# Row statistics on ScalarE, twelve more units turned by VectorE, and weight pieces placed later, in a fused top-k attention and MLP kernel

## The chip, the cores and the metric

The kernel runs on one core of one Trainium2 chip. The metric is the device time of one execution in microseconds (us); the time of a kernel is the median of several runs. A core has TensorE (PE, matmuls into the PSUM banks), VectorE (DVE), ScalarE (ACT), GpSimd (POOL) and SyncE (SP, which here issues nearly all DMAs). Each engine works through its own instructions in the order in which the program issues them, and waits on semaphores for the others.

## What is computed

The inputs are q, k and v of shape (8, 8, 576, 64), a gain g_ln of 512, and two weight matrices, 512 x 2048 and 2048 x 512, which arrive as 64-bit floats. Cut to what matters, the reference is:

```python
scores = q @ k.T / sqrt(64)
kth = np.partition(scores, -32, axis=-1)[..., -32:-31]
scores = np.where(scores >= kth, scores, -1e9)
attn = softmax(scores)
x = heads_side_by_side(attn @ v)              # (8, 576, 512)
mu = np.mean(x, axis=-1, keepdims=True)
var = np.mean((x - mu) ** 2, axis=-1, keepdims=True)
xn = (x - mu) / np.sqrt(var + 1e-06) * g_ln
out = x + np.maximum(xn @ w_ch1, 0.0) @ w_ch2
```

So each query keeps its 32 best keys. Everything is done in 32-bit floats.

## The kernel before

**Units and steps.** A job is one pair of heads of one batch with some of its query tiles; four query tiles have 128 rows and the rest tile has 64. A unit is one query tile of one job: a whole unit holds both heads' scores, 128 x 576 each, and a rest unit puts both heads' 64 rows on one 128 x 576 tile. There are 128 whole and 32 rest units. The main loop (L1201) makes one step per unit, and a few more at the end. In step n the program issues, in this order and to the queues of all engines: scores of unit n + 2 (`scores`, L373: PE matmuls L398, ScalarE copies L379), the selection of unit n on VectorE in four rounds of maxima and replacements (`select`, L422, with L441, L427, L433), the mask of unit n - 1 (`mask`, L487: ScalarE L490, then GpSimd's subtraction L493), its exponentials with their sums (`weigh`, L495: ScalarE L501), the turning of an older unit's weights, and values, projections and weights as they come due. At the end of a step `halve` (L407) makes the larger and the smaller half of the next unit's scores on VectorE (L419, L420), which the selection works on, and `watch` (L456) has GpSimd note a doubt in the selection (L460).

**The early steps.** In the steps up to 8 the mask and the exponentials of unit n - 1 are both in step n, and its transposes right behind them. `values` (L620: PE, L625 and L632) stands before the scores while n is at most `gives_first`, which is 9, and after them later (L1222, L1228).

**Turning.** The weights of a unit have to stand with keys on the partitions before they meet v. Either PE transposes them (L559, eight 128 x 128 transposes for a whole unit, with ScalarE's copies L571 out of PSUM), or the unit is "moved" (`move`, L527): VectorE transposes 32 x 32 blocks (L532, two instructions), one DMA writes the result to HBM and, in the step after, four DMAs bring it back into `pt` in the right places (`bring`, L538). 88 units are moved: from the fifth job on, all whole units but the last of their group. The last 64 keys of each unit, the "end keys", are always turned by PE (`turn_ends`, L582 to L592, and a ScalarE copy L602); for a moved unit this happens in step i + 3, right behind the scores and values of that step (L1232). The tiles e that hold the weights have two buffers, so the mask of a later unit waits for these transposes.

**The MLP.** A pair of 128-row tiles of x is a block; there are 18, two of them of rest rows. When a block's attention is complete, `give` (L1149) puts its work into the list `todo`: `rows` (transposes of x, L729), `hidden` (L770) and `project` (L809 in the first block, L927 in the others). `fill` (L269), called eight times a step, pops items from the list as a planned share per call allows; an item at the front that may not run yet holds up all behind it. The planner (`slot`, L1159) spreads what is left evenly over the steps up to coming blocks and keeps a reserve of 4 us for the moment at which a block is given. The last six items left at that moment are put behind the new rows (`at_end`, L1154).

**Statistics.** `Block.stats` (L689) makes each tile's mean and variance on VectorE (L695, L696). In the first block VectorE also subtracts the mean (L698); in the others GpSimd negates it (L701) and adds it (L704). The row may be transposed from the next step on (`centred`, L707). Tiles are done in the step after their last values, behind round 2 of the selection.

**Weights.** The 64-bit weights come in 32 pieces of 128 x 512 (16 for each matrix; `Piece`, L122). A piece is fetched (`fetch`), split (`split`: ScalarE L163, L165, L168, GpSimd's clamp L164 and, for the first matrix, the gain L170), shifted (`shift`: VectorE L176) and joined (`join`: GpSimd L182, L184). `batches` (L200) says which pieces belong to which step: four before the loop, then two and one in turn in steps 0 to 7, none in 8 and 9, two in each of 10 to 17. `weights(n, phase)` (L209) fetches the next step's pieces and splits the first of this step's early in the step; it joins the last step's and splits the second at the end of the step, or, from step 7 on (`LAZY`), in the middle, where the shift stands ahead of it. The first block may use a piece from the step after its join.

Of the kernel before, what the change touches and what calls it, by code (L numbers as in the profile page):

```python
# [29 lines left out]
def compute(  # L30
# [91 lines left out]
    class Piece:  # L122
# [26 lines left out]
        def split(self):  # L149
            i = self.i  # L150
            high = self.raw[:, :, 1].bitcast(FP32)
            if i < NF:
                self.size = hpool.tile([P, DM], U32, tag="h", name="size")[:]
                self.low = wt_rows[:, i % 8]
                homes = ((opool, "o"), (opool, "o"), (rpool, "r"), (rpool, "r"), (xtpool, "xT"))
            else:
                self.size = wt_rows[:, 2 * i % 8].bitcast(U32)
                self.low = wt_rows[:, (2 * i + 1) % 8]
                homes = ((opool, "o"), (opool, "o"), (rpool, "r"))
# [41 lines left out]
    queue = list(pieces)  # L201
    for n in range(-1, NF + 2):
        count = 4 if n < 0 else 1 + (n + 1) % 2 if n < NF // 2 else 0 if n < NF // 2 + 2 else 2
        batches[n], queue = queue[:count], queue[count:]
    assert not queue

    LAZY = 7

    def weights(n, phase):  # L209

        now, before = batches.get(n, []), batches.get(n - 1, [])
        if phase == 0:
            for x in batches.get(n + 1, []):
                x.fetch()
            for x in now[0::2]:
                x.split()
        elif phase == 1:
            for x in before:  # L220
                x.join()
            for x in now[1::2]:
                x.split()

# [38 lines left out]

    loads, sends = Later(), Later()
    brings = {}

    def fill(least=0):  # L269
        tick[0] += 1  # L270
        loads.settle(LOAD_AGE)
        sends.settle(SEND_AGE)
        ends_later.settle(END_AGE)
        fetch_forms(FETCH_AGE)
        owed[0] = min(owed[0] + share[0], 6.0)
        while todo and (not todo[0][3] or todo[0][3]()):
            if owed[0] < todo[0][1] / 2 and least <= 0:
                break
            least -= 1
            pop()  # L280
# [398 lines left out]
    class Block:  # L679
# [9 lines left out]
        def stats(self, i):  # L689
            x = self.x[i]  # L690
            if self.mv is None:
                self.mv = small.tile([P, J, 2], FP32, tag="mv", name="mv")
                self.rstd = small.tile([P, J], FP32, tag="rstd", name="rstd")
            st = brief_small.tile([P, 6], FP32, tag="st", name="st")
            nc.vector.bn_stats(out=st[:], in_=x)  # L695
            nc.vector.bn_aggr(out=self.mv[:, i, :], in_=st[:])  # L696
            if now[0] <= gives_first:
                nc.vector.tensor_scalar_sub(x, x, self.mv[:, i, 0:1])  # L698
            else:
                less = brief_small.tile([P, 1], FP32, tag="less", name="less")  # L700
                nc.gpsimd.tensor_scalar(  # L701
                    less[:], self.mv[:, i, 0:1], -1.0, 0.0, ALU.mult, ALU.add
                )
                nc.gpsimd.tensor_scalar(x, x, 1.0, less[:], ALU.mult, ALU.add)  # L704
            self.step[i] = now[0]

        def centred(self, i):  # L707
            return i in self.step and (now[0] <= gives_first or done(self.step[i]))

# [246 lines left out]
    SUM_AGE, END_AGE, FETCH_AGE, STORE_AGE, LOAD_AGE = 7, 6, 10, 8, 3  # L956
    SEND_AGE = 2
    blocks = []
# [89 lines left out]

    for u in units[EARLY:]:
        u.moved = not u.rest and u is not u.group.units[-1]  # L1050

# [97 lines left out]
    def give(n):  # L1149
        early = not all(map(done, ready))  # L1150
        for blk in gives[n]:
            rows, hidden, project = blk.items()

            at_end = 0 if early else 6  # L1154
            kept, last = todo[: len(todo) - at_end], todo[len(todo) - at_end :]
            assert all(t[0] == "project" for t in last)
            todo[:] = kept + rows + last + hidden + project
# [43 lines left out]
    for n in range(END):  # L1201
# [19 lines left out]
        ahead = due(n) if n else []  # L1221
        if g and n <= gives_first:  # L1222
            values(g)
        if quick:
            take_values(g)
        for x in ahead:
            scores(x)
        if g and n > gives_first:  # L1228
            values(g)
        if n in brings:  # L1230
            brings.pop(n)()
            late_ends = turn_ends(at(n - 3))  # L1232
        if u:
# [23 lines left out]
        if not early:  # L1257
            weights(n, 0)
        fill()
        if mk and not early:  # L1260
            prepare(mk)
# [153 lines left out]
```

## Time and profile before

| | us |
|---|---|
| median of 3 runs | 1619.47 (1617.36 to 1622.83) |
| the profiled execution | 1617.56 |
| its span | 1615.8 |
| PE busy | 1486.2 (92%) |
| VectorE busy | 1397.4 (86%) |
| GpSimd busy | 1084.7 (67%) |
| ScalarE busy | 1076.2 (67%) |

The profile is of one execution. The span runs from the first instruction to the last, and the execution's own time stands 1.8 us above it. Busy times are sums over the span; an engine's idle time costs something only where that engine sets the pace. Matmuls are pipelined and their ends are modelled, so PE's pace is better read from the times at which matmuls start than from their durations. A 32-bit matmul appears as two instructions, a transpose as one. Lines such as L770 are lines of the kernel before.

### The profile page before, as it was taken

The page shows a single profiled execution, that of the slowest core. Times are in us where ns is not written, and L with a number is a line of the kernel's source. Part 1 is how long each engine was busy: PE and PEld are TensorE (multiplying, and loading weights), DVE is VectorE, ACT ScalarE, POOL GpSimd, SP SyncE. Part 2 cuts the span into 40 slices and gives each one's busy share as a digit, 9 for nine tenths or more (in the row PEclk, how much of TensorE's full clock was granted, in tenths as well). Part 3 has the DMA queues.
Part 4 walks back from the last instruction along what each step waited for, and adds up shares of the span by engine and source line. Part 5 has one row for each costly group of instructions (what it writes and reads, how often), then busy time and mean ns, then how long its engine had stood idle before and what let it go on. Part 6 is the DMA issues. An engine that isn't in the chain of part 4 may idle for free.

```text
span 1615.8 us, 27078 instructions
## 1 busy us (share of the span) xinstructions
PE 1486.2 (92%) x7770; PEld 1124.1 (70%) x7770; DVE 1397.4 (86%) x3971; ACT 1076.2 (67%) x2984; POOL 1084.7 (67%) x1489
## 2 busy tenths in 40 slices
PE   3548978899989899999999999999999999999997
PEld 1335536567757677777777777777777777778886
DVE  7877879999999999999999999999999999982000
ACT  5776776676767686777776767677677776763311
POOL 6984887866647576777766768586767675756334
PEclk9768989899989999999999999999999999999999
DMA  8423455553656455545564556446564455522211
GB/s 214 128 75 115 146 154 124 173 159 115 189 140 189 127 159 155 172 146 145 163 189 135 142 137 189 153 131 169 136 189 150 130 163 160 167 81 86 70 36 54
DMA packets 367205, 228.27 MB, mean 141 GB/s; under 512 B 248772, under 2 KB 337352, under 8 KB 367048
## 3 DMA queue, kind: packets, MB, share of 16 engines
q1 hardware_dynamic: 362312, 225.86, 48.5%
q8 instruction: 64, 1.05, 0.3%
q10 hardware_dynamic: 4736, 0.59, 0.2%
q14 instruction: 93, 0.76, 0.2%
HBM read 154.01 MB, written 72.35 MB: 140 GB/s over the span
## 4 chain that ended last, share of the span: by engine, by line
PE 73%; POOL 10%; DVE 7%; ACT 6%; DMA 2%; issue 1%; SPq 0%; POOLq 0%; ACTq 0%; DVEq 0%
PE hps L770 27%; PE ops L927 22%; PE scps L398 9%; PE av L625 7%; POOL e L493 3%; PE tp L559 3%; PE av L632 2%; DVE m L441 2%; DVE hi L427 2%; POOL w L184 2%; ACT sc L379 1%; ACT e L490 1%; PE tp L729 1%; ACT e L501 1%; POOL wt L182 1%
## 5 line engine op out<-in xcount | busy, mean ns | idle before, releaser
L493 POOL TENSOR_TENSOR e<-e,sc 128x576 f32<-128x576 f32 x288 | 419.7, 1475 | 352.9 <-ACT e L490 352.5
L770 PE MATMUL hps<-xT,w 128*128 128x256 f32 x2304 | 544.0, 386 | 0.7 <-ACT xT L732 0.7
L770 PEld LDWEIGHTS hps<-xT,w 128*128 128x128 f32 x2304 | 429.7, 193 | 69.5 <-issue 11.8
L441 DVE MAX8 m<-hi 128x8 f32<-128x296 f32 (+1 forms) x1152 | 470.9, 444 | 0.1
L427 DVE MATCH_REPLACE8 hi<-m,hi 128x288 f32<-128x288 f32 (+1 forms) x864 | 378.0, 443 | 0.0
L927 PE MATMUL ops<-w,h 128*128 128x256 f32 x1360 | 323.1, 384 | 0.0
L501 ACT ACTIVATE e<-e,m 128x576 f32<-128x576 f32 x288 | 224.3, 779 | 119.0 <-POOL e L493 117.5
L927 PEld LDWEIGHTS ops<-w,h 128*128 128x128 f32 x1360 | 253.0, 193 | 37.9 <-issue 4.2
L379 ACT COPY sc<-scps 128x288 f32<-128x288 f32 x576 | 199.4, 407 | 101.4 <-PE scps L398 68.5
L490 ACT ACTIVATE e<-sc,m 128x576 f32<-128x576 f32 x288 | 212.3, 770 | 47.8 <-PE tp L592 47.8
L420 DVE TENSOR_TENSOR lo<-sc 128x576 f32<-128x576 f32 (+1 forms) x160 | 167.6, 1048 | 0.0
L419 DVE TENSOR_TENSOR hi<-sc 128x576 f32<-128x576 f32 (+1 forms) x160 | 142.9, 893 | 12.2 <-POOL watched L460 8.3
L625 PE MATMUL av<-pt,vb 128*64 128x256 f32 (+2 forms) x1088 | 147.0, 411 | 4.9 <-ACT r L644 4.3
L793 ACT ACTIVATE h<-hps 128x512 f32<-128x512 f32 x144 | 85.6, 595 | 80.4 <-PE hps L770 80.1
L532 DVE STREAM_TRANSPOSE sc<-e 128x512 f32<-128x512 f32 x176 | 114.3, 686 | 25.6 <-ACT e L501 25.6
L398 PE MATMUL scps<-kT,late_qT 64*128 64x288 f32 (+3 forms) x832 | 124.8, 413 | 7.5 <-ACT x L644 4.2
L927 PE MATMUL ops<-wt,s 128*128 128x256 f32 x544 | 128.6, 381 | 0.0
L559 PE MATMUL tp<-ident,e 128*128 128x128 f32 x448 | 75.7, 297 | 53.3 <-ACT e L501 53.3
L625 PEld LDWEIGHTS av<-pt,vb 128*64 128x64 f32 x1088 | 75.3, 141 | 62.2 <-issue 11.5
L433 DVE MAX8 hi<-lo 128x8 f32<-128x288 f32 x288 | 117.8, 445 | 0.0
L398 PEld LDWEIGHTS scps<-kT,late_qT 64*128 64x128 f32 (+1 forms) x832 | 70.4, 169 | 61.5 <-issue 23.8
L398 PE MATMUL scps<-kT,qT 64*128 64x288 f32 x512 | 92.8, 460 | 21.0 <-DVE qT L328 11.6
(104 smaller groups left out, 1893.4 us busy)
## 6 DMA issues: line engine op xcount, KB each, us to landing
turned<-sc SPq DMA_DIRECT2D x88, 512.0 KB, 2.8
pt<-turned SPq DMA_DIRECT2D x352, 128.0 KB, 2.8
w<-forms SPq DMA_DIRECT2D x136, 256.0 KB, 4.2
vb<-in_v_dram SPq DMA_DIRECT2D x68, 288.0 KB, 3.8
raw<-in_moe_w_ch_dram SPq DMA_DIRECT2D x32, 512.0 KB, 4.7
kT<-kept SPq DMA_DIRECT2D x36, 288.0 KB, 3.4
kin<-in_k_dram SPq DMA_DIRECT2D x128, 72.0 KB, 2.5
kept<-kT SPq DMA_DIRECT2D x32, 288.0 KB, 3.0
```

The source lines that it names most:

```text
L379: nc.scalar.copy(u.sc[:, t, s * HALF : (s + 1) * HALF], made[s][t][:, 0:HALF])
L398: nc.tensor.matmul(ps[i * R : i * R + ql, o : o + width], qT[r, q0 : q0 + ql], kT[r, k0 : k0 + width], start=True, stop=True,)
L419: nc.vector.tensor_tensor(hi, a, b, ALU.max)
L420: nc.vector.tensor_tensor(lo, a, b, ALU.min)
L427: nc.vector.match_replace(x, m[:, t, :], x, LOWEST)
L441: nc.vector.max(m[:, t, :], u.hi[:, t, 0:width])
L490: nc.scalar.activation(u.e[:, t], u.sc[:, t], AF.Relu, bias=u.edge[:, t : t + 1], scale=-STEEP)
L493: nc.gpsimd.tensor_tensor(u.e[:, t], u.e[:, t], u.sc[:, t], ALU.subtract)
L501: nc.scalar.activation(u.e[:, t], u.e[:, t], AF.Exp, bias=u.bias[:, t : t + 1], scale=-scale, accum_out=g.den[:, col : col + 1],)
L625: nc.tensor.matmul(av[h * D : (h + 1) * D, 0 : g.nq], vb[:, h * (J + 1) + c, :], g.blocks[:, h, 0 : g.nq // 32, c, :], start=(c == 0), sto ...
L770: nc.tensor.matmul(ps[0][:, side * N : (side + 1) * N], w1[:, c, f * P : (f + 1) * P], self.xT[:, c, 0:N], start=(c == 0), stop=(c == NC - 1),
L927: nc.tensor.matmul(bank[name][:, 0:Q], a(j), rhs, start=first and j == 0, stop=(j == G - 1), skip_group_check=not first,)
```

## The change

It has five parts.

1. **Statistics.** From the second block on, ScalarE copies the tile onto itself while it sums it (into the place of the variance), multiplies the sum by 1/512 to the mean, and, five fills later, squares the centred tile into a PSUM bank while it sums the squares, and multiplies that sum by 1/512. GpSimd subtracts the mean in one instruction. A row may be transposed six fills after its statistics were issued, in place of the next step.
2. **Turning.** The last whole unit of a group without a rest unit is moved too, from the third batch on, for every other pair of heads, if the next job does not begin with a rest unit: 12 units more, 100 in all.
3. **Weight pieces.** One piece a step in steps 0 to 7, none in 8, one in 9, then two a step in 10 to 18, and the last in 19. From step 9 on (`LATE`) a step's pieces are all split at the end of the step, behind shift and join of the last step's, and the next step's are fetched behind that. The shift stands right before the join in all steps, at the end. The last four pieces of the first matrix use the same homes for their parts as those of the second.
4. **Order on PE.** Values stand behind the scores in all steps but that of the first block's last group. The end keys of a moved unit are turned behind the first fill of the step.
5. **Rows.** Ten remaining items instead of six are put behind a new block's rows.

```diff
@@ split
-            if i < NF:
+            if i < 3 * NC:
@@ batches
-    for n in range(-1, NF + 2):
-        count = 4 if n < 0 else 1 + (n + 1) % 2 if n < NF // 2 else 0 if n < NF // 2 + 2 else 2
+    for n in range(-1, NF + 4):
+        count = 4 if n < 0 else 1 if n < NF // 2 else 0 if n == NF // 2 else 1 + (n > 9)
         batches[n], queue = queue[:count], queue[count:]
-    LAZY = 7
+    LATE = NF // 2 + 1
     def weights(n, phase):
         now, before = batches.get(n, []), batches.get(n - 1, [])
+        coming = batches.get(n + 1, [])
         if phase == 0:
-            for x in batches.get(n + 1, []):
+            for x in coming if n < LATE else []:
                 x.fetch()
-            for x in now[0::2]:
+            for x in now[0::2] if n < LATE else []:
                 x.split()
         elif phase == 1:
             for x in before:
+                x.shift()
+            for x in before:
                 x.join()
-            for x in now[1::2]:
+            for x in now if n >= LATE else now[1::2]:
                 x.split()
+            for x in coming if n >= LATE else []:
+                x.fetch()
@@ fill
         sends.settle(SEND_AGE)
+        squares.settle(SQUARE_AGE)
@@ Block.stats
+            mean, var = self.mv[:, i, 0:1], self.mv[:, i, 1:2]
             if now[0] <= gives_first:
                 st = brief_small.tile([P, 6], FP32, tag="st", name="st")
                 nc.vector.bn_stats(out=st[:], in_=x)
                 nc.vector.bn_aggr(out=self.mv[:, i, :], in_=st[:])
                 nc.vector.tensor_scalar_sub(x, x, mean)
             else:
-                nc.gpsimd.tensor_scalar(
-                    less[:], self.mv[:, i, 0:1], -1.0, 0.0, ALU.mult, ALU.add
-                )
-                nc.gpsimd.tensor_scalar(x, x, 1.0, less[:], ALU.mult, ALU.add)
-            self.step[i] = now[0]
+                nc.scalar.activation(x, x, AF.Copy, accum_out=var)
+                nc.scalar.mul(mean, var, 1.0 / DM)
+                nc.gpsimd.tensor_scalar(x, x, 1.0, mean, ALU.mult, ALU.subtract)
+                def square():
+                    ps = brief("squares")
+                    nc.scalar.activation(ps[:], x, AF.Square, accum_out=var)
+                    nc.scalar.mul(var, var, 1.0 / DM)
+                squares.add(square)
+            self.step[i] = tick[0]
@@ centred
-            return i in self.step and (now[0] <= gives_first or done(self.step[i]))
+            return i in self.step and (
+                now[0] <= gives_first or tick[0] - self.step[i] >= CENTRE_AGE
+            )
-    SEND_AGE = 2
+    SEND_AGE, CENTRE_AGE, SQUARE_AGE = 2, 6, 5
@@ which units are moved
-    for u in units[EARLY:]:
-        u.moved = not u.rest and u is not u.group.units[-1]
+    for j, nj in zip(jobs, jobs[1:] + [None]):
+        for u in units[max(j.first, EARLY) : j.last + 1]:
+            u.moved = not u.rest and (
+                u.i < j.last or (j.b > 1 and j.hp % 2 == 0) and nj is not None and not units[nj.first].rest
+            )
@@ give
-            at_end = 0 if early else 6
+            at_end = 0 if early else 10
@@ the step
-        if g and n <= gives_first:
+        if quick:
             values(g)
-        if quick:
             take_values(g)
         for x in ahead:
             scores(x)
-        if g and n > gives_first:
+        if g and not quick:
             values(g)
         if n in brings:
             brings.pop(n)()
-            late_ends = turn_ends(at(n - 3))
...
         fill()
+        turned_before = at(n - 3)
+        if turned_before and turned_before.moved:
+            late_ends = turn_ends(turned_before)
         if mk and not early:
             prepare(mk)
             mask(mk, 0)
...
-        if n >= LAZY:
-            for x in batches.get(n - 1, []):
-                x.shift()
...
-        if n >= LAZY:
-            weights(n, 1)
...
         if nxt:
             halve(nxt)
-        if n < LAZY:
-            for x in batches.get(n - 1, []):
-                x.shift()
-            weights(n, 1)
+        weights(n, 1)
```

More of the change, by code (lines that the diff above doesn't have):

```diff
@@ L201, in compute @@
     queue = list(pieces)
-    for n in range(-1, NF + 2):
-        count = 4 if n < 0 else 1 + (n + 1) % 2 if n < NF // 2 else 0 if n < NF // 2 + 2 else 2
+    for n in range(-1, NF + 4):
+        count = 4 if n < 0 else 1 if n < NF // 2 else 0 if n == NF // 2 else 1 + (n > 9)
         batches[n], queue = queue[:count], queue[count:]
+    batches = {n: x for n, x in batches.items() if x}
     assert not queue
-    LAZY = 7
+    LATE = NF // 2 + 1
     def weights(n, phase):
         now, before = batches.get(n, []), batches.get(n - 1, [])
+        coming = batches.get(n + 1, [])
         if phase == 0:
-            for x in batches.get(n + 1, []):
+            for x in coming if n < LATE else []:
                 x.fetch()
-            for x in now[0::2]:
+            for x in now[0::2] if n < LATE else []:
                 x.split()
@@ L264, in compute @@
     sums_later, ends_later, stores = Later(), Later(), Later()
-    loads, sends = Later(), Later()
+    loads, sends, squares = Later(), Later(), Later()
     brings = {}
@@ L693, in stats @@
                 self.rstd = small.tile([P, J], FP32, tag="rstd", name="rstd")
-            st = brief_small.tile([P, 6], FP32, tag="st", name="st")
-            nc.vector.bn_stats(out=st[:], in_=x)
-            nc.vector.bn_aggr(out=self.mv[:, i, :], in_=st[:])
+            mean, var = self.mv[:, i, 0:1], self.mv[:, i, 1:2]
             if now[0] <= gives_first:
-                nc.vector.tensor_scalar_sub(x, x, self.mv[:, i, 0:1])
-            else:
-                less = brief_small.tile([P, 1], FP32, tag="less", name="less")
-                nc.gpsimd.tensor_scalar(
-                    less[:], self.mv[:, i, 0:1], -1.0, 0.0, ALU.mult, ALU.add
-                )
-                nc.gpsimd.tensor_scalar(x, x, 1.0, less[:], ALU.mult, ALU.add)
-            self.step[i] = now[0]
+                st = brief_small.tile([P, 6], FP32, tag="st", name="st")
+                nc.vector.bn_stats(out=st[:], in_=x)
+                nc.vector.bn_aggr(out=self.mv[:, i, :], in_=st[:])
+                nc.vector.tensor_scalar_sub(x, x, mean)
+            else:
+                nc.scalar.activation(x, x, AF.Copy, accum_out=var)
[7 more added lines that the diff above has]
+            self.step[i] = tick[0]
         def centred(self, i):
-            return i in self.step and (now[0] <= gives_first or done(self.step[i]))
+            return i in self.step and (
+                now[0] <= gives_first or tick[0] - self.step[i] >= CENTRE_AGE
+            )
         def inverse(self):
```

## The prediction

> **What bounds the kernel now.** I read the busy time by stretches first. I cut it where the work changes; a step is one unit's selection, found by the maxima of L433. Columns: stretch, its length, then busy time (and instructions) of PE, weight loads, VectorE (DVE), ScalarE (ACT), GpSimd (POOL), granted clock, DMA share, GB/s.
>
> ```profile
> 0.00:121.00 121.00, 55.05 (x218) 34.76 (x219) 92.74 (x257) 82.35 (x200) 96.51 (x102) 0.79 0.52 139
> 121.00:246.00 125.00, 104.90 (x477) 64.56 (x477) 96.65 (x267) 90.20 (x235) 91.85 (x98) 0.89 0.47 138
> 246.00:560.00 314.00, 284.75 (x1506) 206.73 (x1501) 310.81 (x889) 217.42 (x634) 212.88 (x290) 0.94 0.53 152
> 560.00:1440.00 880.00, 875.51 (x4768) 674.94 (x4768) 874.84 (x2493) 635.17 (x1798) 604.29 (x855) 1.00 0.54 154
> 1440.00:1606.00 166.00, 165.97 (x815) 143.10 (x813) 22.39 (x70) 49.19 (x117) 75.44 (x143) 1.00 0.20 61
> ```
>
> There are four regimes. Up to 121 us and again to 246 us no engine is full. From 246 to 560 us VectorE is full (310.8 of 314) and PE loses 29 us. From 560 us to the end PE never stands still. There VectorE reads full too, so which of them leads? Steps 28 to 56 (322 to 552 us) take 8.2 us each; steps 56 to 156 (552 to 1424 us), with the same selections but more MLP matmuls per step, take 8.7. VectorE can do 8.2, so PE leads. VectorE's surplus is in halving, which stretches: 0.74 and 0.75 us for its two instructions at 104.28 us, on average 0.96 and 1.13. So time from 560 us on is PE work, and before it is whatever holds up the steps.
>
> Second view, the chain of work, 70 to 96 us (start, length, what):
>
> ```profile
> 71.84 0.77 ACT e L501 x2
> ...
> 72.65 2.20 PE tp L559 x8
> 74.86 0.21 PE tp L592
> 75.07 3.56 PE av L625 x16
> 78.63 0.63 PE av L632 x2
> 79.26 1.22 PE scps L398 x8
> 80.48 0.98 ACT sc L379 x3
> ...
> 81.66 1.38 ACT e L490 x2
> ...
> 84.71 0.77 ACT e L501 x2
> ```
>
> It is a loop: exponentials, transposes, values, next scores, their copies, the mask, exponentials again: 12.9 us. The loops without values take 10.1 (61.76 to 71.84, 84.71 to 94.80).
>
> Third view, the waits of 121 to 246 us, and the groups by line:
>
> ```profile
> DVE wt L176 <- POOL wt L164: 21.0, 6, 5.7
> ACT sign L168 <- POOL w L184: 18.7, 6, 4.7
> ```
>
> ```profile
> L559 PE MATMUL tp<-ident,e 128*128 128x128 f32 x448 | 75.7, 297 | 53.3 <-ACT e L501 53.3
> L532 DVE STREAM_TRANSPOSE sc<-e 128x512 f32<-128x512 f32 x176 | 114.3, 686 | 25.6 <-ACT e L501 25.6
> L695 DVE BATCH_NORM_STATS2 st<-x 128x6 f32<-128x512 f32 x32 | 21.6, 674 | 34.8 <-ACT x L644 34.8
> L696 DVE BATCH_NORM_AGGREGATE mv<-st 128x2 f32<-128x6 f32 x36 | 6.6, 182 | 1.2
> ```
>
> VectorE stops in its selections for weight pieces' shifts, because the clamp it needs (L164) stands behind GpSimd's joins.
>
> **The change, part by part.** The sum is made against the profiled execution's own 1617.56 us (span 1615.8 and 1.8 around it); the median shown is 1619.47.
>
> *First steps (0 to 121 us): -12.* Values now stand behind the scores on PE in the three early steps that have them (from 53, 75 and 98 us). That takes 3.56 + 0.63 = 4.2 us out of the loop; the matmuls then run beside mask, subtraction and exponentials (79 to 85 us), which PE awaits anyway. A loop of 8.7 us is less than VectorE's share: busy 58.1 of 75 us over the six steps from 46 to 121 us, 9.7 a step. So each saves about 12.9 - 9.7 = 3.2, together 9.6. One piece a step instead of two and one removes four pieces here; each is 0.6 + 0.9 + 1.35 + 1.5 = 4.3 us of GpSimd, on the chain only before 50 us: I take 2.4. Ends: 4 (the next wait takes the loop's place) and 16.
>
> *Weight stage (steps 9 to 20, 121 to 254 us, 133 us): -11.* All splitting and joining stands at the step's end, with the shift a whole step after its clamp: the 21.0 us of VectorE's waits go. What is late next is GpSimd. It has 20 pieces there instead of 16: 16 at 3.4 and 4 at 4.3 us, masks of eight whole and four half units 28.5, and some 10 of small work: 110 us. VectorE has 104.7. So 133 can fall by 22 at most. GpSimd worked 96.5 of 133 and never without gaps; its joins now also stand behind the watch of the step (L460), which needs the last selection. I take half, 11. Against: the last piece is joined in step 20 instead of 18, so the first block ends near step 21 instead of 19; a step of about 8.5 us lost in place of any gain is the other end.
>
> Here joins come to stand beside halving. The halving at 116.47 us took 1.95 us beside GpSimd's subtraction, against 0.75 alone. The Trainium skill, "SBUF — State Buffer", section "Who interferes with whom", goes further: a VectorE instruction with two SBUF inputs and a reading GpSimd instruction exclude each other for a whole instruction. By that rule each of some 11 steps would pay up to a join, 1.35 us, or 15 us in all, and this term would be about +4 instead of -11. By the row it is 1.2 us a step, and hidden where GpSimd is the later of the two anyway, so the term stays.
>
> *246 to 560 us: -4.* VectorE leads. Six tiles' statistics leave it (6 x 0.86 = 5.1); one pair of transposes comes (two of L532, 1.29 us with their overlap, at 1057.61). Ends 0 and 5.
>
> *Twelve more units turned by VectorE.* Each takes eight transposes from PE. Four of them hold it 0.44 us (from 1066.16 to the next matmul at 1066.60), so a unit is 0.87 and with the switches about 1.0. Eleven of the twelve are turned after 560 us: -11. VectorE pays 1.29 each, 14, and gives back 0.86 for each of some 25 tiles there, 21: it does not become the bound. Each unit also issues five DMAs on SP (one 512 KB, four of 128 KB, 2.8 us to land each); they are done a step before values read them, if the step's 8.7 us hold. Ends: -13, and -2 where VectorE leads after all.
>
> The Trainium skill's "Perfetto Trace Analysis", section "Identifying the Most-Contended Engine", speaks against this term: busy matmul time says little, weight loads' share is to be read. That is 675 of 880 us, 77%, so PE would have room and the term would be 0. The row decides: in the tail 128 hidden matmuls take 27.79 us, 0.216 each, without a gap, and the matmuls between 560 and 1440 us keep that spacing.
>
> *Statistics on ScalarE: 0, hidden.* 34 tiles: a Copy and a Square with sums (each 0.68 as L168, plus 0.19 to read the sum, as L501's) and two small multiplies (0.2): 2.1 us each, 73 in all, less 24 copies of 0.6. ScalarE goes from 635 to about 675 of 880 in the long stretch. No row shows Copy or Square with a sum; the ends are the plain 0.6 and L501's 0.97. GpSimd loses 34 x 0.2.
>
> *End keys later, rows: +3.* The ends' transposes go behind a fill of about 0.75 us of MLP; the mask needs their e buffer, so it starts that much later. Exponentials end a good 8 us before VectorE's transposes, which covers it. Rows come in front of ten instead of six remaining items, and become eligible two fills later. Where only some nine items (4 us) are left, at steps 76 and 156, PE runs out 1 to 2 us earlier each time: +3 (0 to 8). At steps 32 and 44 VectorE leads and it costs nothing.
>
> Sum: -12 - 11 - 4 - 11 + 3 = -35, so 1582.6 by the profiled execution; the median stands 1.9 above that, 1584.5. I predict **1584**.
>
> **Rivals.**
> - *GpSimd holds the weight stage.* For: 96.5 of 133 busy, and joins wait for the watch. Against: 21 us of waits that do go. Then -8 early, 0 there: 1617.6 - 8 - 4 - 11 + 3 = 1598 (1593 to 1611).
> - *The weight stage falls to GpSimd's floor* and the first steps give 16: -22 - 16 - 4 - 11 + 1: about 1567.
> - *Late turned units.* If the DMAs of a group's last unit land after values ask, PE waits. Price: issue and landing, 1.7 + 2.8 = 4.5 us each at most, 11 times 50; at 3 us, 33 of the 35 us are gone: within 0.3%. Against: a step lies between.
> - *Slower: ScalarE becomes the link.* Place: its queue in 560 to 1440 us, where the mask waits for the ends behind a fill and then the new Copy and Square stand before the copies that free PE's banks. PE waits there for almost nothing today. A wait of w per step costs 100 w; it decides from w = 0.35 on; at 0.5, 1633. For: ScalarE's masks already waited 44 us for these transposes (L592) in that stretch. Against: 245 us of idle time there.
>
> **How the numbers follow.** Forecast 0.50 (1573 to 1592), GpSimd 0.23, the floor 0.10, late units 0.05, slower 0.12. All but the last two are faster by over 0.3% (about what a measurement can tell from no change), except a sliver of GpSimd's: faster 0.82, same 0.07, slower 0.11. The range from 1564 to 1611 leaves out some 0.2.
>
> **What would show it.** Right: no wait of VectorE for L164, steps 3, 5 and 7 near 10 us, the steps up to 56 done some 27 us earlier, PE full from there on with 96 transposes fewer. Wrong: PE waits for ScalarE after 560 us, a stretch to step 20 no shorter than 240 us, or VectorE waiting for ScalarE's exponentials.

## The result, and the profile after

| kernel | median of runs, us | ratio to before, 95% interval |
|---|---|---|
| before, beside it | 1618.41 | 1 |
| changed | 1644.87 (1641.26 to 1647.86) | 1.0157 (1.0142 to 1.0171) |

The change makes the kernel 26 us slower; 1584 with a range of 1564 to 1611 had been forecast. The profiled execution took 1647.86 us, span 1646.0. It stands 3 us above the median, so the profile shows 30 us more than before where the medians show 26.

Busy time by the same stretches, columns as before:

```profile
0.00:121.00 121.00, 62.79 (x267) 39.27 (x267) 101.66 (x286) 84.56 (x212) 83.92 (x95) 0.83 0.50 133
121.00:246.00 125.00, 99.55 (x445) 60.19 (x445) 105.89 (x252) 92.91 (x240) 104.97 (x107) 0.90 0.55 154
246.00:560.00 314.00, 280.11 (x1456) 204.98 (x1454) 292.98 (x853) 216.08 (x639) 203.42 (x277) 0.93 0.53 151
560.00:1440.00 880.00, 860.43 (x4608) 656.11 (x4609) 868.65 (x2419) 647.32 (x1882) 614.52 (x824) 0.99 0.57 163
1440.00:1606.00 166.00, 159.77 (x765) 133.15 (x764) 41.63 (x122) 65.91 (x181) 79.62 (x120) 0.96 0.25 79
```

Up to 121 us PE and VectorE did more than before. Between 246 and 560 us VectorE, which had been full (310.8), did only 293.0. From 560 to 1440 us PE, which had stood for 4.5 us, stood for 20, and its mean granted clock fell from 1.00 to 0.99. The time at which a step begins, set against the kernel before, says where the time went (in us, from one profiled execution of each kernel). Below are the changed kernel and four experiments that follow: the statistics alone on the kernel before (`stats_alone`); the changed kernel with the statistics of before (`late_rows`); that with pieces two a step (`late_two`); and the changed kernel with two mendings (`add_two`).

| step | before, us | changed | stats_alone | late_rows | late_two | add_two |
|---|---|---|---|---|---|---|
| 9 | 121.0 | -17.2 | +2.2 | -17.5 | -15.3 | -14.8 |
| 20 | 246.2 | -17.0 | +0.1 | -15.4 | -19.8 | -20.8 |
| 21 | 254.0 | -6.7 | +0.7 | -12.1 | -20.0 | -21.1 |
| 29 | 332.4 | +2.4 | +2.5 | -1.4 | -21.5 | -19.5 |
| 60 | 589.3 | +5.2 | +1.0 | -0.7 | -21.7 | -18.0 |
| 102 | 949.3 | +15.3 | +9.5 | +2.2 | -16.5 | -9.1 |
| 152 | 1388.4 | +20.3 | +18.2 | -1.1 | -19.9 | -8.6 |
| end | 1615.8 | +30.3 | +30.0 | -2.0 | -20.5 | -6.2 |

Two separate losses are to be seen in the column of the changed kernel. A lead of 17 us at step 20 is gone by step 29. And from step 60 to the end 25 us more are lost, 15 to step 152 and 10 in the tail, where PE had set the pace.

For the first, the waits of the changed kernel in 121 to 246 us (us in total, times, longest):

```profile
PE ops L822 <- POOL w L184: 12.4, 8, 4.3
DVE wt L176 <- POOL wt L164: 10.8, 7, 3.2
```

VectorE's wait for the clamp is halved, not gone, and now PE waits for joined pieces, in the first block's second matmuls. By the trace the last join ends at 249.2 us; before, it ended at 241.3, although the steps now run 17 us earlier. The last join before, and in the changed kernel (start, length):

```profile
240.05 1.27 POOL L184 TENSOR_TENSOR w<-wt,sign 128x512 f32<-128x512 f32 x1
```

```profile
247.95 1.27 POOL L184 TENSOR_TENSOR w<-wt,sign 128x512 f32<-128x512 f32 x1
```

Then, until 321 us, PE stands 8.4 us for the first "form" (sums of parts of the second matrix, which GpSimd makes after the first block has used that matrix, and which the later blocks fetch back from HBM):

```profile
PE ops L940 <- DMA w<-forms: 8.4, 1, 8.4
```

For the second, PE's waits in 560 to 1640 us, first before, then after:

```profile
PE av L625 <- ACT r L644: 4.3, 2, 2.3
PE xo L667 <- ACT oT L640: 0.2, 1, 0.2
```

```profile
PE xo L672 <- ACT oT L645: 8.4, 7, 2.9
PE hps L783 <- ACT xT L745: 5.1, 4, 1.7
PE tp L742 <- ACT squares L712: 3.5, 6, 1.1
...
PE tp L742 <- POOL x L708: 1.7, 2, 1.3
```

ScalarE, for which PE had waited 4.5 us in all, now holds it in several places, some 20 us. One of them in the timeline of the changed kernel (start, length, engine, line; in brackets the idle time before and what ended it):

```profile
917.07 0.70 PE L637 MATMUL av<-pt,ends 128*128 128x256 f32 x2
...
917.95 3.99 POOL L708 TENSOR_SCALAR x<-x,mv 128x512 f32<-128x512 f32 x2
...
919.20 0.78 ACT L495 ACTIVATE e<-sc,m 128x576 f32<-128x576 f32 x1
...
919.99 0.60 ACT L712 ACTIVATE squares<-x 128x512 f32<-128x512 f32 x1
...
921.90 0.20 POOL L465 TENSOR_TENSOR watched<-hi,m 128x2 f32<-128x2 f32 x1
921.97 0.60 ACT L712 ACTIVATE squares<-x 128x512 f32<-128x512 f32 x1 [1.03 <-POOL x L708]
...
922.05 1.41 POOL L498 TENSOR_TENSOR e<-e,sc 128x576 f32<-128x576 f32 x1
...
922.83 0.76 ACT L495 ACTIVATE e<-sc,m 128x576 f32<-128x576 f32 x1
923.50 0.35 ACT L645 COPY oT<-av 128x256 f32<-128x256 f32 x1
...
923.90 0.29 PEld L672 LDWEIGHTS xo<-ident,oT 128*128 128x128 f32 x2 [2.97 <-ACT oT L645]
923.90 0.69 PE L672 MATMUL xo<-ident,oT 128*128 128x128 f32 x2 [2.57 <-ACT oT L645]
```

The values (`av`) were summed at 917.8. Their copy `oT` stands in ScalarE's order behind two Squares, and the second Square waits 1.03 us for GpSimd's centring of its tile. GpSimd needs 3.99 us for two tiles. So `oT` is copied at 923.50, and PE stands for 2.57 us. GpSimd's own work comes late too, behind the centring: the small subtraction `watched`, and the mask's subtraction (L498), which starts at 922.05, 2.07 us after ScalarE's part of the mask has ended.

The groups of the changed kernel (busy us, mean ns of one, idle before):

```profile
L564 PE MATMUL tp<-ident,e 128*128 128x128 f32 x352 | 59.0, 297 | 41.2 <-ACT e L506 39.8 <-ACT sc L384 1.3
L537 DVE STREAM_TRANSPOSE sc<-e 128x512 f32<-128x512 f32 x200 | 130.8, 686 | 50.3 <-ACT e L506 25.0 <-POOL e L498 19.8 <-issue 4.5
```

```profile
L708 POOL TENSOR_SCALAR x<-x,mv 128x512 f32<-128x512 f32 x30 | 61.0, 2042 | 11.4 <-ACT mv L707 9.4 <-DMA qin<-in_q_dram 1.3
...
L706 ACT ACTIVATE x<-x 128x512 f32<-128x512 f32 x30 | 18.5, 617 | 0.0
L712 ACT ACTIVATE squares<-x 128x512 f32<-128x512 f32 x30 | 17.7, 591 | 12.8 <-POOL x L708 12.8
```

The change shows in the counts: 96 transposes have left PE, 24 are added on VectorE, and the Copy and the Square take 0.62 and 0.59 us. The row to stop at is L708. The same row of before (L704, GpSimd's centring with the mean made negative) was:

```profile
L704 POOL TENSOR_SCALAR x<-x,less 128x512 f32<-128x512 f32 x30 | 23.9, 797 | 3.1
```

One tile, one column of scalars, multiply and add: 0.80 us. With multiply and subtract: 2.04.

### The profile page after: what moved, and what is told of

Same layout as the page of the kernel before. It is cut to its first block, busy times and chain, and to the rows that moved or that the text cites. A ratio compares the mean times of both kernels' runs of the same rounds, so it can differ in the third digit from the quotient of the medians.

```text
span 1646.0 us, 27080 instructions
## 1 busy us (share of the span) xinstructions
PE 1492.6 (91%) x7674; PEld 1119.7 (68%) x7674; DVE 1410.8 (86%) x3927; ACT 1112.8 (68%) x3164; POOL 1105.1 (67%) x1455
## 5 line engine op out<-in xcount | busy, mean ns | idle before, releaser
L498 POOL TENSOR_TENSOR e<-e,sc 128x576 f32<-128x576 f32 x288 | 424.1, 1489 | 366.5 <-ACT e L495 365.8
L783 PE MATMUL hps<-xT,w 128*128 128x256 f32 x2304 | 556.7, 391 | 12.7 <-ACT xT L745 8.0
L783 PEld LDWEIGHTS hps<-xT,w 128*128 128x128 f32 x2304 | 433.6, 196 | 93.4 <-issue 16.5
L940 PE MATMUL ops<-w,h 128*128 128x256 f32 x1360 | 326.9, 386 | 9.1 <-DMA w<-forms 8.4
L424 DVE TENSOR_TENSOR hi<-sc 128x576 f32<-128x576 f32 (+1 forms) x160 | 156.2, 976 | 23.1 <-POOL watched L465 19.2
L537 DVE STREAM_TRANSPOSE sc<-e 128x512 f32<-128x512 f32 x200 | 130.8, 686 | 50.3 <-ACT e L506 25.0
L425 DVE TENSOR_TENSOR lo<-sc 128x576 f32<-128x576 f32 (+1 forms) x160 | 173.7, 1086 | 0.0
L403 PE MATMUL scps<-kT,qT 64*128 64x288 f32 x512 | 96.1, 469 | 20.6 <-DVE qT L333 11.5
L940 PEld LDWEIGHTS ops<-wt,s 128*128 128x128 f32 x544 | 100.2, 191 | 16.9 <-issue 3.5
```

What stands on the lines that cost most here:

```text
L403: nc.tensor.matmul(ps[i * R : i * R + ql, o : o + width], qT[r, q0 : q0 + ql], kT[r, k0 : k0 + width], start=True, stop=True,)
L424: nc.vector.tensor_tensor(hi, a, b, ALU.max)
L425: nc.vector.tensor_tensor(lo, a, b, ALU.min)
L498: nc.gpsimd.tensor_tensor(u.e[:, t], u.e[:, t], u.sc[:, t], ALU.subtract)
L783: nc.tensor.matmul(ps[0][:, side * N : (side + 1) * N], w1[:, c, f * P : (f + 1) * P], self.xT[:, c, 0:N], start=(c == 0), stop=(c == NC - 1),
L940: nc.tensor.matmul(bank[name][:, 0:Q], a(j), rhs, start=first and j == 0, stop=(j == G - 1), skip_group_check=not first,)
```

## The experiments

**First round: each part undone in the changed kernel.** Theory Q then was: ScalarE's statistics delay what PE waits for. The rivals put the loss on another part. The edits are the lines of the diff above, turned back.

`undo_stats`: the statistics' part turned back, and with it the age from which a row may be transposed.

> The changed kernel with the statistics by VectorE and GpSimd as before, rows eligible from the next step. Theory Q (ScalarE's statistics hold rows back: PE stands at the rows of blocks given with little work left, and falls to half clock): about 8 us less, 1637, with fewer half-clock spells after 1440 us. Rival V again (VectorE is the bound in the stretches of eight steps): its 34 statistics at 0.86 us come back there, and it is slower by 5 to 15, 1650 to 1660.

Measured 1616.9, 0.9988 (0.9979 to 0.9998): 28 us come back, the whole loss. Theory Q had forecast 8, from rows that come late; rival V falls.

`undo_weights`: pieces and `weights` as before.

> The changed kernel with the weight pieces, their splits, shifts and joins placed as before. Theory W (the first block ends two steps later, its last projections wait for joins, the forms of the second matrix come too late and steps 20 to 30 lose what the early steps gained): steps 20 to 30 take about 100 us instead of 112, PE's wait of 8.4 us for the forms is gone, the waits of VectorE for the clamp (21 us before) come back; total about 1632 to 1636. Rival S (the late pieces are harmless, what is lost in steps 20 to 30 comes from statistics and order): it loses the 5 us of the early spread and gains nothing, about 1650.

Measured 1638.6, 1.0110 (1.0089 to 1.0131): 6 us, less than theory W's 9 to 13.

`undo_moved`: 88 moved units again.

> The changed kernel with 88 moved units instead of 100; all else as changed. Theory V (VectorE is the bound in the eight steps of each batch that hold the query tiles 2 and 3, where the twelve units lie): those stretches fall by about 2.3 us each, six of them, so 1645 falls to about 1631, and the half-clock spells of PE in them go. Rival P (the recorded prediction: PE sets the pace from 560 us on, each unit is worth 1 us): it rises by about 11, to 1656.

Measured 1638.0, 1.0118 (1.0101 to 1.0135): rival P falls, and theory V gets half of its 14 us.

`undo_ends`: the end keys ahead of the fill again.

> The changed kernel with the end keys of moved units turned right behind scores and values again. Theory E (behind the fill the ends wait for MLP matmuls, the mask waits for the ends, and the mask's delay is felt): 5 to 10 us less, about 1637, and ScalarE's waits for these transposes fall from 52 to about 44 us in the long stretch. Rival (a wait that other work covers): within 2 us of 1645.

Measured 1638.3, 1.0115 (1.0098 to 1.0131), as theory E had it. Each of the three gives back 6 to 7 us; only the statistics account for the whole loss.

**Second round: the statistics alone, and what in them costs.** `stats_alone` is the kernel before with the statistics' part added; `values_order` is the kernel before with the order of values and scores alone.

> The kernel before with the statistics' part of the change alone: Copy with sum, mean and Square on ScalarE, the row tile's transposes six fills later; all else as before. Theory Q (the statistics' four instructions in ScalarE's order delay what PE and GpSimd wait for, whatever else is changed): undoing them took 28 us off the changed kernel, so alone they should add about the same to 1618 us: 1640 to 1648 us. Rival I (they cost because the moved units, the spread pieces and the late end keys have filled the same queues; each of the three, undone alone, gave back 6 to 7 us): with those three undone 20 us should be gone, and the time is 1622 to 1630 us.

Measured 1648.7, 1.0180 (1.0156 to 1.0204). Theory Q holds and rival I falls: the statistics cost 30 us with nothing else changed. They give nothing where VectorE leads (step 20 +0.1, step 60 +1.0), and take everything from step 60 on.

> The changed kernel with VectorE's and GpSimd's statistics of before, but the row tile's transposes still held for six fills after the statistics. Theory Q: the work on ScalarE is the cost and the hold is not: 1613 to 1621 us, as with the statistics wholly undone (1617). Rival M (rows that come later take away what PE does during its waits): 1635 to 1645 us.

```diff
         def centred(self, i):
-            return i in self.step and (now[0] <= gives_first or done(self.step[i]))
+            return i in self.step and (
+                now[0] <= gives_first or tick[0] - self.step[i] >= CENTRE_AGE
+            )
```

(against `undo_stats`). Measured 1616.2, 0.9987 (0.9977 to 0.9997): the hold of six fills costs nothing.

> The changed kernel without the Square, its PSUM bank and the mean of squares; the reciprocal deviation is made from a constant, so the rows are not scaled by their deviation. Copy with sum, mean, and GpSimd's wait for the mean stay. If the cost is ScalarE's time (theory Q, in proportion): half of the 28 us comes back, 1628 to 1634 us. If it is the fifth PSUM bank or the late Square: nearly all, 1616 to 1622 us. If it is that rows wait through GpSimd for ScalarE's mean: nearly nothing, 1640 to 1645 us.

```diff
-                def square():
-                    ps = brief("squares")
-                    nc.scalar.activation(ps[:], x, AF.Square, accum_out=var)
-                    nc.scalar.mul(var, var, 1.0 / DM)
-                squares.add(square)
```

Measured 1623.5, 1.0031 (1.0020 to 1.0041), between the first two forecasts: 21 of the 28 us go with the Square, its bank and its wait for the centred row, more than its share of ScalarE's time.

> The kernel before with only the order of values and scores in the first steps changed, all else as before. In the changed kernel with the old pieces the steps from 9 to 60 begin 4 us earlier than before. If PE keeps that lead to the end: 1613 to 1616 us. If the later stage takes it back: 1617 to 1620 us.

Measured 1614.1, 0.9968 (0.9958 to 0.9979): 4 us. They are won by step 9; the lead is 6 to 7 us from step 20 to 60, and some 2 of it go in the tail.

**Third round: length or place of the Square, and the pieces.**

> The changed kernel with the Square on one of the 512 columns, so that its place in ScalarE's order, its PSUM bank and the scaling after it stay and its length goes; the variance is that of one column, so the rows are scaled wrongly. Leaving the Square, its bank and its scaling out altogether gave 1623.5 us. Theory Q, by length: the Square's duration is what costs, so nearly all of that comes back, 1623 to 1628 us. Rival B (the bank, taken from the ring of five that scores, transposes and sums of values use, and the place in the order): the time stays at 1638 to 1645 us.

```diff
-                    nc.scalar.activation(ps[:], x, AF.Square, accum_out=var)
+                    nc.scalar.activation(ps[:, 0:1], x[:, 0:1], AF.Square, accum_out=var)
```

Measured 1634.1, 1.0106 (1.0089 to 1.0123): halfway, so both theories fall in their pure form. Its waits show what stayed:

```profile
ACT squares L712 <- POOL x L708: 15.5, 13, 1.7
```

> As late_rows (statistics of before with the hold, 1616.2 us), but from step 8 on two pieces in a step, so that the last piece is joined two steps earlier. In late_rows the last piece is joined at 243.8 us against 241.3 us in the kernel before, although the steps there begin 15 to 20 us earlier; PE then stands 3.5 us for the piece and, near 308 us, 9.6 us for the first form. Theory G (the pieces' end on GpSimd sets the end of that stage): the lead survives step 29 at more than 8 us and the time is 1603 to 1610 us. Rival F (GpSimd's work until there is full in any order, and the joins only push other work back): the lead is gone again by step 29, 1614 to 1619 us.

```diff
-        count = 4 if n < 0 else 1 if n < NF // 2 else 0 if n == NF // 2 else 1 + (n > 9)
+        count = 4 if n < 0 else 1 if n < NF // 2 else 2
```

Measured 1596.9, 0.9864 (0.9848 to 0.9881), the best kernel so far. The last join ends at 222.4 us (243.8 in `late_rows`), PE no longer stands for the first form, and the lead at step 29 is 21.5 us and stays. Theory G is right in its mechanism; the time lies 6 us below its range. The last join:

```profile
221.14 1.26 POOL L184 TENSOR_TENSOR w<-wt,sign 128x512 f32<-128x512 f32 x1
```

The stretch from 121 to 246 us:

```profile
121.00:246.00 125.00, 111.27 (x551) 71.80 (x550) 123.44 (x304) 101.83 (x264) 113.11 (x122) 0.95 0.57 162
```

VectorE is busy for 123.4 of 125 us: the stage is at the floor that VectorE's selections set.

> The changed kernel with the statistics on VectorE and GpSimd and the weight pieces of before; values' order, 100 moved units, late end keys and the hold of six fills stay. Values' order alone has the steps 6 to 7 us early from step 9 on and ends at 1614.1 us; with the pieces undone the other edits kept 4 to 5 us of it at step 60. If the pieces are what took it back, and the moved units and end keys save what late_rows shows from step 60 on (about 1 us): 1609 to 1614 us. If the moved units or end keys cost without the statistics too: 1615 to 1620 us.

Measured 1611.2, 0.9951 (0.9934 to 0.9967), as forecast if the late pieces are what takes the early lead back: what is left of the change gains 7 us.

> As all_but_stats_and_pieces, but with 88 moved units as before instead of 100. If the 12 more moved units bring PE work off its path without the statistics (8 transposes of 0.11 us each and their switches): 3 to 11 us slower than all_but_stats_and_pieces. If VectorE's side of it takes that back, as with the statistics, where undoing it gained 7 us: the same within 3 us, or faster.

Measured 1613.9, 0.9972 (0.9962 to 0.9982): by the medians the twelve more moved units are worth 2.7 us, and with two intervals that overlap a little this is at the edge of what can be told. One reason why it is not 11 is seen in two stretches of eight steps with whole units alone, 92 to 100 and 132 to 140, in the kernel before (92 to 100 alone), then with 88 and with 100 moved units (columns as in the stretches above):

```profile
859.17:932.42 73.25, 73.25 (x404) 56.16 (x406) 73.18 (x214) 54.05 (x152) 51.02 (x70) 1.00 0.50 141
```

```profile
852.15:926.20 74.05, 74.05 (x409) 56.81 (x410) 73.98 (x213) 53.98 (x154) 51.10 (x73) 1.00 0.48 136
1206.46:1278.83 72.37, 72.37 (x398) 55.63 (x400) 72.30 (x212) 53.12 (x152) 51.24 (x76) 1.00 0.50 144
```

```profile
855.98:930.94 74.96, 73.95 (x399) 56.23 (x400) 74.89 (x217) 51.53 (x149) 51.91 (x74) 1.00 0.52 152
1208.98:1282.67 73.69, 72.99 (x395) 55.35 (x396) 73.62 (x216) 51.33 (x149) 50.73 (x76) 1.00 0.52 154
```

With 88, PE and VectorE are both full. With 100, these stretches hold two transposing pairs more, VectorE alone is full, and they are 0.9 and 1.3 us longer. The step times say what became of PE's relief: from step 60 on, the five stretches that hold ten of the twelve units cost 4.2 us with 100 (steps 72 to 80, and so on every twenty steps), the twelve steps between two of them save 7.6, and the last step and the tail 2.3. So 5.6 us of it came, by one execution of each. But the kernel with 88 is 4.9 us ahead at step 60, half of that won in steps 52 to 60, which hold the other two units; where the rest comes from is open.

**Fourth round: what the Square waits for.** Theory S: the subtracting form on GpSimd is slow and, through the Square's wait, holds ScalarE.

> The changed kernel with the row tile centred on GpSimd by adding the negative mean (ScalarE's small instruction multiplies by -1/512) in place of subtracting the mean; the number of instructions and their order stay. In the changed kernel GpSimd's centring takes 2.04 us a tile (34 of them) where the kernel before took 0.80 us, and ScalarE's Square waits for it (12.8 us in all). Theory S (the subtracting form is what is slow, and through the Square's wait holds ScalarE): the centring falls to 0.8 us, the Square's wait is nearly gone, and the time is 1630 to 1638 us. Rival P (GpSimd is slow for another reason, the mean's place or ScalarE beside it): 2.0 us stays and the time is 1642 to 1647 us.

```diff
-                nc.scalar.mul(mean, var, 1.0 / DM)
-                nc.gpsimd.tensor_scalar(x, x, 1.0, mean, ALU.mult, ALU.subtract)
+                nc.scalar.mul(mean, var, -1.0 / DM)
+                nc.gpsimd.tensor_scalar(x, x, 1.0, mean, ALU.mult, ALU.add)
```

Measured 1628.9, 1.0067 (1.0050 to 1.0084): one sign and one operation take 16 us off, 1 us more than theory S allowed. GpSimd's centring in the changed kernel and in this one (shortest/median/longest, ns):

```profile
L708 POOL TENSOR_SCALAR x<-x,mv x30: 1991/1998/3114, 233.3 to 1578.3; 128x512 f32<-128x512 f32 x30
...
  ACT squares L712: 12.8, 13
```

```profile
L708 POOL TENSOR_SCALAR x<-x,mv x30: 687/692/1800, 233.1 to 1559.7; 128x512 f32<-128x512 f32 x30
```

The second line of the first fence is who waited for it (us, times). Where the mean lies and who makes it are the same in both, so it is the operation that makes 2.00 of 0.69 us. PE's waits for ScalarE's copy from 560 us on are halved:

```profile
PE xo L672 <- ACT oT L645: 4.3, 7, 1.3
```

That all 16 us come through the Square's wait is not shown: the shorter centring also lets GpSimd go on sooner to the mask's subtraction and PE to the centred rows. The next run takes away the wait alone.

> As tiny_square (1634.1 us), but the one-column Square reads a constant column and no longer the centred row, so that ScalarE never waits there for GpSimd; its PSUM bank and its place in the order stay. The rows are scaled wrongly. Theory S (ScalarE's wait for GpSimd, 15.5 us in tiny_square, is what is left of the Square's cost there): 1623 to 1627 us, as without the Square. Rival B (the bank of the ring of five): 1632 to 1636 us.

```diff
-                    nc.scalar.activation(ps[:], x, AF.Square, accum_out=var)
+                    nc.scalar.activation(ps[:, 0:1], ident[:, 0:1], AF.Square, accum_out=var)
```

Measured 1628.1, 1.0050 (1.0034 to 1.0067): 6 us below `tiny_square`. With the short Square, ScalarE's wait was worth 6 us; 4.6 remain above `no_square`, 1 us beyond what theory S gave.

> As tiny_square (1634.1 us), but the one-column Square writes a column in SBUF and takes no PSUM bank; it still waits for the centred row. The rows are scaled wrongly. Theory S (the wait): 1632 to 1636 us. Rival B (the bank): 1623 to 1627 us. Half and half would show in both this and tiny_const.

```diff
-                    ps = brief("squares")
-                    nc.scalar.activation(ps[:], x, AF.Square, accum_out=var)
+                    nc.scalar.activation(self.rstd[:, i : i + 1], x[:, 0:1], AF.Square, accum_out=var)
```

Measured 1640.7, 1.0140 (1.0122 to 1.0157). Giving the bank back gains nothing, so rival B falls; but it is 6.7 us slower than `tiny_square`, which theory S did not allow either, and this stays unexplained.

> The changed kernel with nothing but the pieces' order changed: two pieces a step from step 8 on, as in late_two (1596.9 us), with the statistics on ScalarE as in the change. In late_two this took 19.3 us off late_rows. If what the pieces cost and what the statistics cost add up: 1623 to 1628 us. If ScalarE's statistics also take back a lead that is won early: 1635 to 1645 us.

The edit is that of `late_two`. Measured 1623.5, 1.0035 (1.0020 to 1.0049): 21 us, so the pieces' cost is there with either kind of statistics.

**Last round: both mendings, and the best kernel.**

> The changed kernel with both mendings: the mean added in its negative on GpSimd (add_form took 16 us off the changed kernel) and two pieces a step from step 8 on (after_two took 21 us off). The statistics stay on ScalarE. If the two causes are apart: 1605 to 1611 us. If both live from the same waits: 1614 to 1622 us. ScalarE's statistics are worth having only if this is below late_two's 1597 us, which I do not expect: 9 to 12 us of them stay in ScalarE's order.

Measured 1609.2, 0.9944 (0.9927 to 0.9960). Apart the mendings are worth 15.9 and 21.4 us, together 35.7: two causes, nearly independent. `late_two`, with VectorE's statistics, is still 12.3 us faster.

> As late_two (statistics of before, two pieces a step from step 8 on; 1596.9 us), but with the end keys turned ahead of the fill again, as before. With the statistics on ScalarE this edit alone was worth 7 us. If the late end keys cost only because ScalarE's mask then stands among the statistics: 1595 to 1599 us. If they cost by themselves: 1588 to 1593 us.

The edit is that of `undo_ends`. Measured 1593.9, 0.9848 (0.9831 to 0.9864), 1.5% faster than the kernel before and the best of all. It lies between what the two theories gave: end keys late cost some 3 us by themselves, though 0.2% between two runs of this kind is at the edge of what can be told.

## Why the prediction was wrong

The forecast of 1584 was missed by 61 us. By steps of the sum:

- *Statistics on ScalarE: 0, hidden.* This is the step that failed most: 30 us alone. It counted ScalarE's time against ScalarE's idle time (73 us beside 245). But what counts, as at 917 us, is what stands behind the Copy and the Square in the order: `oT`, `xT`, the next mask. It let GpSimd's centring stand at its old price ("GpSimd loses 34 x 0.2"), though the operation was another; it went from 0.80 to 2.04 us, 42 us more for 34 tiles, and it stood between two ScalarE instructions. `add_form` gives 16 us for that. The prediction's own first sign of being wrong, PE waiting for ScalarE after 560 us, is what came. Of the rest, `add_two` against `late_two` shows 12 us that ScalarE's statistics cost even so.
- The rival *ScalarE becomes the link* named the place and the queue rightly and had 0.12. Its price did not fit: 15 us in the 92 steps from 60 to 152 is 0.16 a step, where it needed 0.35 to decide, and 10 us more went in the tail. That the kernel got slower took the late pieces as well. It did not name GpSimd's share.
- *Weight stage: -11.* It gave no lead (-17.2 at step 9, -17.0 at step 20), which is what the rival *GpSimd holds the weight stage* had there, and then took the earlier lead away: the nine steps to 29 lost 19.4 us. The row "the last piece is joined in step 20 instead of 18" stood in the text as the other end, priced at one step, 8.5 us. In truth two things wait for the last piece, the first block's second matmuls and, through that block, the first form's DMA, and each costs a stop of 8 to 10 us. With the last piece two steps earlier (`late_two`) the stage gives 5 us (-15.3 to -19.8) and takes nothing afterwards; more is not to be had, since VectorE is full there.
- *First steps: -12.* 15 to 17 us came. The split was wrong: the order of values is worth 4 (`values_order`), not 9.6, and the pieces taken out of the first steps some 13 (step 9 at -17.2 in the changed kernel, at -3.9 with the pieces undone), not 2.4.
- *Twelve more units turned by VectorE: -11.* About 2.7 (`best_88`). The step that failed is the first view's: "VectorE can do 8.2, so PE leads". The two stretches that it compares hold unlike shares of rest units, 8 of 28 steps against 20 of 100, and rest steps are short on VectorE. In steps with whole units alone VectorE is full too (73.2 of 73.3 us in steps 92 to 100 of the kernel before, shown above), so what was taken from PE was put there on an engine that had no room; PE's relief came only in the steps between.
- *246 to 560 us: -4.* Nothing came: in `stats_alone` step 20 is at +0.1 and step 60 at +1.0.
- *End keys later, rows: +3.* `late_two_ends` measured 3.1, but this is luck: the 3 were put down to the rows, and the end keys to nothing ("which covers it"). Its edit moves the end keys alone, and they cost 3; the ten items behind the rows were not tried by themselves.

So of 61 us, 16 are the subtracting form, 21 the late pieces, 12 the rest of ScalarE's statistics, and 12 what the moved units and VectorE's relief did not bring (8 and 4). The shares are differences between several kernels, and that they close is in part luck: the first steps gave 3 to 5 us more than forecast and the weight stage, even with the pieces early, 6 less.

What stays open: why undoing the moved units or the late end keys gave 7 us each in the changed kernel, where without ScalarE's statistics undoing the first costs 2.7 and undoing the last gives 3, and why `tiny_sbuf` is slower than `tiny_square`. (The pieces put back give much the same in both, 6 us there and 5 between `late_rows` and `all_but_stats_and_pieces`.) All the runs that are left open have the slow centring in them, and where its waits fall shifts with any edit; that is argued, not shown. The Square's place in the order, kept full but with the wait moved, was not tried, and neither was the adding form without the Square, so how much of the 16 us each of its two ways is worth is open.

## What to carry to other kernels

Before work is moved to an engine with idle time, look at what stands behind it in that engine's order and at whom it waits for; here the chain ScalarE, GpSimd, ScalarE put one engine's delay into the other's queue. When an instruction's operation changes, even from add to subtract, take no duration over from the old one. When work is spread to remove waits, look at when its last piece ends, not at the waits: here the last join 20 us earlier was worth 20 us.

## What the runs showed of the hardware

GpSimd's centring of a 128 x 512 tile took 0.69 us with multiply and add and 2.00 us with multiply and subtract. The Trainium skill, "GPSIMD Engine Reference", section "Engine selection", calls instructions with one input roughly line-rate there; the adding form, beside the 0.67 us that VectorE took for the statistics (L695) of a tile of the same shape, agrees with that, and the subtracting one, with the same single input tile, takes 2.9 times as long.

The granted TensorE clock dropped after short stops of PE. Windows of the changed kernel around the stop shown above (stretch, length, PE busy, granted clock, DMA share, GB/s):

```profile
920.00:923.40 3.40, 1.34 (x7) 1.00 0.37 94
923.40:926.80 3.40, 2.90 (x10) 0.50 0.84 137
926.80:930.20 3.40, 3.40 (x21) 1.00 0.70 194
```

A stop of 2.57 us, 2.06 of them in a window in which PE was still busy for 1.34 of 3.40 us, was followed by 3.4 us at half clock. PE was busy for 2.90 of them, so an estimated 1.5 us more were lost. Such spells came also at 732, 1282, 1456 and 1582 us, 24 us in all with PE busy for 21, an estimated 10 us that is part of what the kernel lost from step 60 on. With the adding form two spells, 10 us, were left. The kernel before had none between 563 and 1610 us. The Trainium skill, "TensorE: Matmul & The Clock Gate", section "What's actually happening", has the clock fall after at least one idle window of about 3.4 us; here a window that was 39% busy was enough, so the threshold lies higher than wholly idle.
